# The two-bank PSUM tile gets a place of its own and takes M's first block; the last output tile goes out in two halves

## The chip, the cores and the metric

The kernel runs on one core of one Trainium2 chip. What counts is the device time of one execution in microseconds (us). Several executions were timed, and one more was taken by the hardware profiler. The engines are called as the profile calls them: PE is TensorE (matmuls and transposes), PEld its weight loads, DVE is VectorE, ACT is ScalarE, POOL is GpSimd, and SP (SyncE) issues the DMAs.

## What is computed

Three blocks follow each other: a causal attention with a bias from a running sum, an expert layer of two products, and a second layer with a softmax-weighted activation and a norm.

```python
# q, k, v: (4, 8, 576, 64); s: (4, 8, 576)
scores = scale * q @ k^T                       # causal mask
scores = scores + minimum(-(cum_i - cum_j), 0) # cum = cumsum(max(s, 0))
attn_out = softmax(scores) @ v
x = attn_out as (2304, 512)

a = x @ w1; b = x @ w2                         # w1, w2: (512, 1024)
x = ((a * b) @ w3) @ w_out                     # w3: (1024, 1024), w_out: (1024, 512)

h = x @ w_in                                   # w_in: (512, 1024)
solu = h * softmax(h)
ln = (solu - mean) / sqrt(var + 1e-6) * g_ln
out = ln @ w_out2                              # (2304, 512)
```

The weights come as 64-bit floats and are made 32-bit on the chip.

## The kernel before

**Precision and words.** Every product is made of three matmuls on fp32r parts: a high part (`hi`, a copy on ACT, L93) and a low part (`lo`, a subtraction, L98, on DVE or POOL). Names end in `h` or `l`, or H and L, for the parts. A 64-bit weight block is loaded into `stage`, made 32-bit by `to_f32` (ACT L340, DVE L346, L347, L351), and split by L93 and L98 into `W` (w1 and w2), `w3h`/`w3l`, and so on. `pump` (L393 on) takes converted blocks in turn; inside the attention it is pinned behind the last score reduction and exponential of part 0 (`behind`, set in `softmax_tile`).

**Attention.** A loop over steps (`for st, (h, ph) in enumerate(steps)`, L541 on) does head h's scores in three parts (`qk_part`, matmuls `sc` at L169, L177, L178; DVE reduces with L186, ACT exponentiates with L190), its normalisation (L218, L219, ACT L226, DVE L228), the transposes of an earlier head `ph` (`tr` L247, copied to `PT` by DVE L95 or ACT L93) and the product with v (`av` L275). Two operations per head split q and k into parts `QK` (ACT L93, POOL L98). From step 10 the matmuls of `a` and `b` (units `ab_unit`, L303, 12 matmuls of 288 columns each) fill in between; ACT copies `a` (L315) and DVE multiplies `b` with it into `g_sb` (L323), which goes to DRAM (`g_scr`).

**PSUM.** Up to step 10 there are a pool psA of two tiles of two banks (`bigtile`) and psB of four tiles of one bank (`smalltile`). At step 11 these are let go, and psE (one tile of two banks) and psF (six of one bank) take their place. `bigtile` serves part 0 of a head's scores and `av`; `smalltile` all else. A tile in a new pool can be written when those that lay in its banks have been read.

**M.** The product w3 @ w_out is made once (`m_unit`, eight blocks of 24 matmuls at L626), so that the second half of the kernel multiplies `g` with M (`x`, L710). Each block's high part goes to `MH`, its low part to `ML`. Before, psC (X, Y, Z, W, one bank each) and psD (four banks) are opened behind psE and psF, and M's blocks take psD's. Meanwhile the DVE splits `gl`, words of `w_in` (`IB11l` and so on) and the last blocks of w3.

**The rest.** For each pair of token tiles: `x`, then `h_pair` (`hX`, `hY`, `hZ`, `hW`, L742, a scheme with seven products for eight), softmax, norm, a transpose (by DMA; by PE for the last two tiles), and `out_unit` (`o`, 24 matmuls of 512 columns at L836, one ACT copy, one store of 256 KB). Tile `o` has one buffer.

**Order.** The program is written in the order of these loops, and a scheduler then sets each engine's own queue from its planned times and from the pools. Lines such as

```python
with tc.issue_after(last_tr[0].ins):
```

pin an instruction behind another. So a change of pools can move instructions on PE, DVE, ACT and SP far from the lines that it edits. Inside an engine the queue is executed in order.

Of the kernel before, what the change touches and what calls it, by code (L numbers as in the profile page):

```python
# [8 lines left out]
F32 = mybir.dt.float32  # L9
# [3 lines left out]
AF = mybir.ActivationFunctionType  # L13
ALU = mybir.AluOpType
AX = mybir.AxisListType
PSUM = bass.MemoryType.PSUM
# [10 lines left out]
def tile_attention_moe(  # L27
# [15 lines left out]
    nc = tc.nc  # L43
    B, H, D, _, S = qkT.shape
    NH = B * H
    T, DM = out.shape
# [3 lines left out]
    KF = DF // 128  # L50
# [6 lines left out]
    for i in (2, 3, 1, 4, 0):  # L57
# [3 lines left out]

    dram = ctx.enter_context(tc.tile_pool(name="dram", bufs=1, space=DRAM))
    ps_ctx = ExitStack()
    PSP = [
        ps_ctx.enter_context(tc.tile_pool(name="psA", bufs=2, space=PSUM)),
        ps_ctx.enter_context(tc.tile_pool(name="psB", bufs=4, space=PSUM)),
# [15 lines left out]
    def bigtile(name):  # L82
        return PSP[0].tile([128, 2, 512], F32, tag="A", name=name)

    def smalltile(name):
        return PSP[1].tile([128, 512], F32, tag="B", name=name)

# [404 lines left out]
    for i in range(2):  # L492
# [14 lines left out]
        out=wmask[:, S - 128:S], in_=wmask[:, S - 128:S], pattern=[[-1, 128]],  # L507
# [36 lines left out]
    for st, (h, ph) in enumerate(steps):  # L544
        for _ in range(NF.get(st, 0)):
            fill.extend(ab_unit(*units.pop(0)))
        left = len(fill)
        if st == 11:
            ps_ctx.close()
            PSP[:] = [  # L550
                ps_ctx.enter_context(tc.tile_pool(name="psE", bufs=1, space=PSUM)),
                ps_ctx.enter_context(tc.tile_pool(name="psF", bufs=6, space=PSUM)),
            ]

        def F(share):
            while fill and len(fill) > left * (1 - share):
                fill.pop(0)()

        if h is not None:
            if NQ <= h + 2 < NH:  # L560
                load_head(h + 2)
            qk_part(h, 0)
        if st > 1:
            pump(PUMP.get(st, 0))
        if h is not None:
            qk_part(h, 1)
            qk_part(h, 2)
        F(FS)
        if h is not None:
            normalise(h)  # L570
        if ph is not None:
            for part in range(4):
                tr_part(ph, part)
        if late:
            with tc.issue_after(last_tr[0].ins):
                for fn in late.pop():
                    fn()
        if h is not None:
            if h % 2 == 1:
                load_v(h // 2)  # L580
            if NQ - 2 <= h < NQ:
                t = QK[h % 2] = at.tile([128, 4, S], F32R, tag="QK", bufs=2, name=f"QK{h % 2}")
                aug_rows(t[:, 0], t[:, 3])
            if h + 1 < NH:
                split_qk(h + 1)
            if h + 3 < NQ:
                load_head(h + 3)
                load_aug(h + 3, cumf_scr[h + 3:h + 4])
            if NQ <= h + 2 < NH:
                load_aug(h + 2, cum_scr[h + 2])  # L590
        F(1)
        if ph is not None and ph % 2:
            parts = av_parts(ph // 2)
            if ph < PD or st == len(steps) - 1:
                for fn in parts:
                    fn()
            else:
                late.append(parts)
# [4 lines left out]
    NT = T // 128  # L603
# [15 lines left out]
        w_job(w3L[f, :, 1024 * i:1024 * i + 1024], dst)  # L619

    def m_unit(f):
        ps = smalltile("m")
        for k in range(KF):
            H3, L3 = m_st[f, k // 4]
            for w_, o_ in ((H3, WOH), (H3, WOL), (L3, WOH)):
                nc.tensor.matmul(  # L626
                    ps, w_[:, k % 4], o_[:, k],
                    start=(k == 0 and w_ is H3 and o_ is WOH), stop=(k == KF - 1 and w_ is L3),
                )
        hi(MH[:, f], ps)  # L630
        lo(ML[:, f], ps, MH[:, f])
# [8 lines left out]
    for i in range(8):  # L640
# [8 lines left out]
    behind.clear()  # L649
    right0.close()  # L650
    ps_ctx.close()
    PSP[:] = [
        ctx.enter_context(tc.tile_pool(name="psC", bufs=1, space=PSUM)),
        ctx.enter_context(tc.tile_pool(name="psD", bufs=4, space=PSUM)),
    ]
    HD = DF // 2

    r2 = ctx.enter_context(tc.tile_pool(name="r2", bufs=1, side="right"))
# [39 lines left out]
    def x2_half(c, i):  # L698
        ps = smalltile("x2").rearrange("p (a t) -> p a t", a=2)
        x2_t[c, i] = ps  # L700
        last = None
        for a in range(2):
            m = 2 * i + a
            with ExitStack() as order:
                if last is not None:
                    order.enter_context(tc.issue_after(last.ins))
                for k in range(KF):
                    GH, GL = g_hl[c][k // 2]
                    for w_, g_ in ((MH, GH), (MH, GL), (ML, GH)):
                        last = nc.tensor.matmul(  # L710
                            ps[:, a], w_[:, k, m * 128:m * 128 + 128], g_[:, k % 2],
                            start=(k == 0 and w_ is MH and g_ is GH), stop=(k == KF - 1 and w_ is ML),
                        )
        if i == 1:
            g_hl.pop(c)
# [114 lines left out]

    def out_unit(t):
        LH, LL = lt_t.pop(t)
        ps = smalltile("o")
        for k in range(KF):
            for l_, w_ in ((LH, OH), (LH, OL), (LL, OH)):
                nc.tensor.matmul(  # L836
                    ps, l_[:, k], w_[:, k],
                    start=(k == 0 and l_ is LH and w_ is OH), stop=(k == KF - 1 and l_ is LL),
                )
        o = p2.tile([128, DM], F32, tag="o", bufs=1, name="o")  # L840
        nc.scalar.activation(out=o, in_=ps, func=AF.Copy)
        nc.sync.dma_start(out=out[t * 128:t * 128 + 128], in_=o)

    NCH = NT // 2

    def h_pair(c):
        t0, t1 = 2 * c, 2 * c + 1
        for t in (t0, t1):
            so = p2.tile([128, DF], F32, tag="so", bufs=2, name="so")
            ln_t[t] = so, p2.tile([128, 8], F32, tag="sv", bufs=4, name="sv")  # L850
        h0, h1 = ln_t[t0][0], ln_t[t1][0]
        X, Y, Z, W = (PSP[0].tile([128, HD], F32, tag=n, name=f"h{n}") for n in "XYZW")
        h_mm(X, "A11", "B11", True)
        copy(h0[:, 0:HD], X)
        h_mm(Z, "S1", "T1", True)
        copy(h1[:, HD:], Z)
        h_mm(Y, "A12", "B21", True)
        meet(t0, 0, Y)
        h_mm(X, "S2", "T2", False)
        copy(h0[:, HD:], X)  # L860
        if c + 1 < NCH:
            x2_first(c + 1)
        h_mm(Z, "S4", "B22", False)
        meet(t0, 1, Z)
        ln_exp(t0)
        h_mm(W, "A22", "T4", True)
        h_mm(X, "S3", "T3", False)
        copy(h1[:, 0:HD], X)
        ln_mean(t0)
        meet(t1, 1, X)  # L870
        meet(t1, 0, W)
        ln_exp(t1)
        ln_apply(t0)
# [34 lines left out]
    p2 = ctx.enter_context(tc.tile_pool(name="p2", bufs=1, side="left"))  # L908
    OH = p2.tile([128, KF, DM], F32R, name="OH")
    OL = p2.tile([128, KF, DM], F32R, name="OL")  # L910
    x2_half(0, 0)
    x2_first(0)
    x2_half(0, 1)
# [7 lines left out]
    for c in range(NCH):  # L921
# [8 lines left out]
        last = c == NCH - 1  # L930
# [77 lines left out]
```

## Time and profile before

| | |
|---|---|
| time, median of 3 runs | 732.38 us (731.66 to 733.02) |
| the profiled execution's own time | 732.8 us |
| its span in the trace | 731.1 us |
| mean granted clock of TensorE | 0.995 |
| PE busy | 714.2 us (98%) |
| DVE, ACT, POOL busy | 507.7, 470.4, 95.2 us |
| HBM read, written | 59.04, 20.14 MB |

The span runs from the first to the last event that the profiler saw; the execution's own time has 1.7 us more around it. An engine's busy time is the union of its instructions' times, and for PE the ends of matmuls are modelled, so back-to-back matmuls overlap in the rows: what one costs in a row of its like is the distance of the starts. A wait is put down to the instruction whose end released it last. PEclk is the granted clock as a share of 2.4 GHz.

### The profile page before, as it was taken

The page shows a single profiled execution, that of the slowest core. Times are in us where ns is not written, and L with a number is a line of the kernel's source. Part 1 is how long each engine was busy: PE and PEld are TensorE (multiplying, and loading weights), DVE is VectorE, ACT ScalarE, POOL GpSimd, SP SyncE. Part 2 cuts the span into 40 slices and gives each one's busy share as a digit, 9 for nine tenths or more (in the row PEclk, how much of TensorE's full clock was granted, in tenths as well). Part 3 has the DMA queues.
Part 4 walks back from the last instruction along what each step waited for, and adds up shares of the span by engine and source line. Part 5 has one row for each costly group of instructions (what it writes and reads, how often), then busy time and mean ns, then how long its engine had stood idle before and what let it go on. Part 6 is the DMA issues. An engine that isn't in the chain of part 4 may idle for free.

```text
span 731.1 us, 12896 instructions
## 1 busy us (share of the span) xinstructions
PE 714.2 (98%) x4618; PEld 631.5 (86%) x4618; DVE 507.7 (69%) x1251; ACT 470.4 (64%) x977; POOL 95.2 (13%) x88
## 2 busy tenths in 40 slices
PE   9989998999999999999998999999999999999997
PEld 6669888889899999999997889988888988888886
DVE  7996989898777887822777966675747366563651
ACT  7996878798676777822544735576737465563742
POOL 3051322234121221000000000001000000000000
PEclk9999999999999999999999999999999999999999
DMA  5644555555476655514566933153324252302311
GB/s 124 190 135 132 156 164 146 164 148 127 140 205 184 207 164 175 179 62 161 185 204 201 378 114 101 59 116 87 79 66 102 45 133 68 87 19 68 66 36 43
DMA packets 79827, 95.50 MB, mean 131 GB/s; under 512 B 41418, under 2 KB 52682, under 8 KB 79764
## 3 DMA queue, kind: packets, MB, share of 16 engines
q1 hardware_dynamic: 79764, 94.69, 44.5%
q8 instruction: 36, 0.59, 0.3%
q14 instruction: 27, 0.22, 0.1%
HBM read 59.04 MB, written 20.14 MB: 108 GB/s over the span
## 4 chain that ended last, share of the span: by engine, by line
PE 81%; DVE 9%; DMA 5%; ACT 2%; issue 2%; SPq 0%; DVEq 0%; ACTq 0%
PE x L710 14%; PE o L836 14%; PE a L303 12%; PE b L303 11%; PE av L275 6%; PE hX L742 5%; PE tr L247 5%; DMA stage<-in_w_dram 4%; PE hZ L742 3%; PE sc L178 2%; PE sc L177 2%; PE hW L742 2%; PE hY L742 2%; DVE stage L351 2%; PE sc L169 1%
## 5 line engine op out<-in xcount | busy, mean ns | idle before, releaser
L190 ACT ACTIVATE P<-P,STAT 64x64 f32<-64x64 f32 (+4 forms) x160 | 88.5, 556 | 22.9 <-DVE STAT L186 22.3
L98 POOL TENSOR_TENSOR QK<-qk,QK 64x1152 fp32r<-64x1152 f32 x24 | 66.2, 2759 | 172.9 <-ACT QK L93 172.8
L710 PE MATMUL x<-gl,MH 128*128 128x256 f32 x288 | 80.4, 279 | 0.0
L710 PE MATMUL x<-gh,ML 128*128 128x256 f32 x288 | 80.2, 279 | 0.0
L710 PE MATMUL x<-gh,MH 128*128 128x256 f32 x288 | 79.9, 279 | 0.0
L303 PE MATMUL b<-xT0h,W 128*128 128x288 f32 x256 | 58.4, 301 | 3.5 <-DVE W L98 2.1
L303 PE MATMUL a<-xT0h,W 128*128 128x288 f32 x256 | 59.2, 306 | 0.0
L247 PE MATMUL tr<-ident,P 128*128 128x128 f32 x416 | 54.4, 275 | 3.5 <-DVE STAT L186 2.7
L303 PE MATMUL a<-xT1h,W 128*128 128x288 f32 x256 | 57.6, 300 | 0.0
L836 PE MATMUL o<-OH,lh 128*128 128x512 f32 x144 | 57.0, 396 | 0.2 <-DVE ll L98 0.2
L836 PE MATMUL o<-OH,ll 128*128 128x512 f32 x144 | 57.0, 396 | 0.0
L836 PE MATMUL o<-OL,lh 128*128 128x512 f32 x144 | 57.0, 396 | 0.0
L303 PE MATMUL b<-xT1h,W 128*128 128x288 f32 x256 | 56.4, 295 | 0.0
L710 PEld LDWEIGHTS x<-gl,MH 128*128 128x128 f32 x288 | 54.1, 188 | 1.5 <-DVE gl L98 0.2
L710 PEld LDWEIGHTS x<-gh,MH 128*128 128x128 f32 x288 | 53.9, 188 | 1.1
L710 PEld LDWEIGHTS x<-gh,ML 128*128 128x128 f32 x288 | 54.0, 188 | 0.9
L806 DVE COPY lt<-turned 128x2048 uint16<-128x2048 uint16 x16 | 22.0, 1373 | 45.4 <-DMA turned<-half 45.4
L247 PEld LDWEIGHTS tr<-ident,P 128*128 128x128 f32 x416 | 46.8, 141 | 5.4 <-issue 1.6
L323 DVE TENSOR_TENSOR g_sb<-b,a_sb 128x288 f32<-128x288 f32 x64 | 28.7, 450 | 31.6 <-PE b L303 21.5
L340 ACT ACTIVATE stage<-stage 128x512 f32<-128x512 f32 x56 | 37.1, 679 | 20.5 <-DMA stage<-in_w_dram 18.7
L226 ACT ACTIVATE P<-P,STAT 128x576 f32<-128x576 f32 x64 | 42.7, 717 | 10.5 <-DVE STAT L219 10.4
L315 ACT ACTIVATE a_sb<-a 128x288 f32<-128x288 f32 x64 | 25.7, 403 | 36.3 <-PE a L303 36.0
(191 smaller groups left out, 1984.1 us busy)
## 6 DMA issues: line engine op xcount, KB each, us to landing
stage<-in_w_dram SPq DMA_DIRECT2D x32, 512.0 KB
g_scr<-g_sb SPq DMA_DIRECT2D x32, 288.0 KB
stage<-in_wo_dram SPq DMA_DIRECT2D x16, 512.0 KB
qk<-in_qk_dram SPq DMA_DIRECT2D x24, 288.0 KB
QK<-QK SPq DMA_DIRECT2D x24, 288.0 KB
gl<-g_scr SPq DMA_DIRECT2D x24, 256.0 KB
wf<-wf_scr SPq DMA_DIRECT2D x22, 256.0 KB
out_dram<-o SPq DMA_DIRECT2D x18, 256.0 KB
```

Of the source, the lines that this page charges most:

```text
L98: eng.tensor_tensor(out=dst, in0=src, in1=hi_.bitcast(F32), op=ALU.subtract)
L190: ex = nc.scalar.activation(out=dst, in_=dst, func=AF.Exp, bias=st[0:rows, ti:ti + 1], scale=-1.0, accum_out=st[0:rows, 5 + ti:6 + ti],)
L226: nc.scalar.activation(out=dst, in_=src, func=AF.Copy, scale=r)
L247: last_tr[0] = nc.tensor.transpose(ps[:, 128 * n:128 * n + 128], pt[:, o:o + 128], ident)
L275: nc.tensor.matmul(st["ps"][64 * e:64 * e + 64, 448 + c0:448 + c1], vr[:, j, e], PT[(2 * p + e) % 4][:, o + c0:o + c1], **kw,)
L303: nc.tensor.matmul(ps, w_[:, c, fs], x_[:, c, sl], start=(c == 0 and w_ is WH and x_ is XH), stop=(c == KC - 1 and w_ is WL),)
L315: ab_last[0] = nc.scalar.activation(out=a_sb, in_=ps, func=AF.Copy).ins
L323: ab_last[1] = nc.vector.tensor_tensor(out=g[:, sl], in0=ps, in1=st["a"], op=ALU.mult).ins
L340: nc.scalar.activation(out=high.bitcast(F32), in_=high.bitcast(F32), func=AF.Copy, scale=2.0 ** -112)
L710: last = nc.tensor.matmul(ps[:, a], w_[:, k, m * 128:m * 128 + 128], g_[:, k % 2], start=(k == 0 and w_ is MH and g_ is GH), stop=(k == KF ...
L742: last_h[0] = nc.tensor.matmul(ps, x_[:, k], w_[:, k], start=first and k == 0 and x_ is XH and w_ is WH, stop=k == 1 and x_ is XL, skip_gr ...
L836: nc.tensor.matmul(ps, l_[:, k], w_[:, k], start=(k == 0 and l_ is LH and w_ is OH), stop=(k == KF - 1 and l_ is LL),)
```

## The change

Three things. At step 11 psE is opened at the other end of PSUM (`side="right"`) under a context `big_ctx` of its own, and psF takes the six banks left of it; before, psE lay at the left and psF right of it. M's first block is written to the first bank of the psE tile, and not to a bank of psD; psE stays open until M is done, psC then holds Z and W alone, and X and Y get a pool psG in the place of psE behind M. And `out_unit` makes its last tile (t = 17) in two halves of 256 columns, each with 24 matmuls, a copy of half the width and a store of 128 KB; the second half's matmuls are pinned behind the first's.

```diff
--- before.py
+++ after.py
@@ -61,6 +61,7 @@
 
     dram = ctx.enter_context(tc.tile_pool(name="dram", bufs=1, space=DRAM))
     ps_ctx = ExitStack()
+    big_ctx = ExitStack()
     PSP = [
         ps_ctx.enter_context(tc.tile_pool(name="psA", bufs=2, space=PSUM)),
         ps_ctx.enter_context(tc.tile_pool(name="psB", bufs=4, space=PSUM)),
@@ -548,7 +549,7 @@
         if st == 11:
             ps_ctx.close()
             PSP[:] = [
-                ps_ctx.enter_context(tc.tile_pool(name="psE", bufs=1, space=PSUM)),
+                big_ctx.enter_context(tc.tile_pool(name="psE", bufs=1, space=PSUM, side="right")),
                 ps_ctx.enter_context(tc.tile_pool(name="psF", bufs=6, space=PSUM)),
             ]
 
@@ -619,7 +620,7 @@
         w_job(w3L[f, :, 1024 * i:1024 * i + 1024], dst)
 
     def m_unit(f):
-        ps = smalltile("m")
+        ps = smalltile("m") if f else bigtile("m")[:, 0]
         for k in range(KF):
             H3, L3 = m_st[f, k // 4]
             for w_, o_ in ((H3, WOH), (H3, WOL), (L3, WOH)):
@@ -649,10 +650,9 @@
     behind.clear()
     right0.close()
     ps_ctx.close()
-    PSP[:] = [
-        ctx.enter_context(tc.tile_pool(name="psC", bufs=1, space=PSUM)),
-        ctx.enter_context(tc.tile_pool(name="psD", bufs=4, space=PSUM)),
-    ]
+    psp = {}
+    psp["Z"] = psp["W"] = ctx.enter_context(tc.tile_pool(name="psC", bufs=1, space=PSUM))
+    PSP[1] = ctx.enter_context(tc.tile_pool(name="psD", bufs=4, space=PSUM))
     HD = DF // 2
 
     r2 = ctx.enter_context(tc.tile_pool(name="r2", bufs=1, side="right"))
@@ -830,16 +830,21 @@
 
     def out_unit(t):
         LH, LL = lt_t.pop(t)
-        ps = smalltile("o")
-        for k in range(KF):
-            for l_, w_ in ((LH, OH), (LH, OL), (LL, OH)):
-                nc.tensor.matmul(
-                    ps, l_[:, k], w_[:, k],
-                    start=(k == 0 and l_ is LH and w_ is OH), stop=(k == KF - 1 and l_ is LL),
-                )
         o = p2.tile([128, DM], F32, tag="o", bufs=1, name="o")
-        nc.scalar.activation(out=o, in_=ps, func=AF.Copy)
-        nc.sync.dma_start(out=out[t * 128:t * 128 + 128], in_=o)
+        last = None
+        for c0, c1 in ((0, DM),) if t < NT - 1 else ((0, DM // 2), (DM // 2, DM)):
+            ps = smalltile("o")[:, 0:c1 - c0]
+            with ExitStack() as order:
+                if last is not None:
+                    order.enter_context(tc.issue_after(last.ins))
+                for k in range(KF):
+                    for l_, w_ in ((LH, OH), (LH, OL), (LL, OH)):
+                        last = nc.tensor.matmul(
+                            ps, l_[:, k], w_[:, k, c0:c1],
+                            start=(k == 0 and l_ is LH and w_ is OH), stop=(k == KF - 1 and l_ is LL),
+                        )
+            nc.scalar.activation(out=o[:, c0:c1], in_=ps, func=AF.Copy)
+            nc.sync.dma_start(out=out[t * 128:t * 128 + 128, c0:c1], in_=o[:, c0:c1])
 
     NCH = NT // 2
 
@@ -849,7 +854,7 @@
             so = p2.tile([128, DF], F32, tag="so", bufs=2, name="so")
             ln_t[t] = so, p2.tile([128, 8], F32, tag="sv", bufs=4, name="sv")
         h0, h1 = ln_t[t0][0], ln_t[t1][0]
-        X, Y, Z, W = (PSP[0].tile([128, HD], F32, tag=n, name=f"h{n}") for n in "XYZW")
+        X, Y, Z, W = (psp[n].tile([128, HD], F32, tag=n, name=f"h{n}") for n in "XYZW")
         h_mm(X, "A11", "B11", True)
         copy(h0[:, 0:HD], X)
         h_mm(Z, "S1", "T1", True)
@@ -908,6 +913,8 @@
     p2 = ctx.enter_context(tc.tile_pool(name="p2", bufs=1, side="left"))
     OH = p2.tile([128, KF, DM], F32R, name="OH")
     OL = p2.tile([128, KF, DM], F32R, name="OL")
+    big_ctx.close()
+    psp["X"] = psp["Y"] = ctx.enter_context(tc.tile_pool(name="psG", bufs=1, space=PSUM, side="right"))
     x2_half(0, 0)
     x2_first(0)
     x2_half(0, 1)
```

The scheduler's queues change with it: POOL's order is the same, those of PE, DVE, ACT and SP differ between step 10 and step 20 of the attention, around M, and at the last tile. Three places follow. Lines are one higher in the changed kernel, and a name's number is its tile's.

PE at step 11. `sc_899` is head 9's part 0 (the two-bank tile), `sc_922` its part 1; `sc_957` and `sc_980` are those of head 10. `a_858`, `b_873` and `a_998` are the first of 12 matmuls of their units. Before:

```order
L177 MATMUL sc_899<-QK1_656 128x512
L178 MATMUL sc_899<-QK1_656 128x512
...
L303 MATMUL a_858<-xT0h_130,W00_122 128x288
...
L303 MATMUL b_873<-xT0h_130,W02_124 128x288
...
L177 MATMUL sc_957<-QK0_595 128x512
L178 MATMUL sc_957<-QK0_595 128x512
...
L177 MATMUL sc_922<-QK1_656 128x448
...
L177 MATMUL sc_980<-QK0_595 128x448
...
L303 MATMUL a_998<-xT0h_130,W00_122 128x288
```

and in the changed kernel:

```order
L304 MATMUL a_858<-xT0h_130,W00_122 128x288
...
L304 MATMUL b_873<-xT0h_130,W02_124 128x288
...
L178 MATMUL sc_899<-QK1_656 128x512
L179 MATMUL sc_899<-QK1_656 128x512
...
L178 MATMUL sc_922<-QK1_656 128x448
...
L178 MATMUL sc_980<-QK0_595 128x448
...
L304 MATMUL a_998<-xT0h_130,W00_122 128x288
...
L178 MATMUL sc_957<-QK0_595 128x512
L179 MATMUL sc_957<-QK0_595 128x512
```

`sc_899` has gone behind `a_858` and `b_873`, and `sc_957` from ahead of `sc_922` into `a_998`.

DVE a little later: `W03_125` is the low part of a converted block of w2, `stage_758` and `stage_766` are two blocks on their way, `tr_1050` a bank of transposes, `STAT1_117` and `P_898` the statistics and probabilities of head 9, `b_1013` the unit ahead of `b_1078`. Before:

```order
L186 ISA STAT2_118 128x1
L351 SCALAR_TENSOR_TENSOR stage_766<-stage_766 128x512
L98 TENSOR_TENSOR W03_125<-stage_758,W02_124 128x4x128
L323 TENSOR_TENSOR g_sb_886<-b_1013,a_sb_1011 128x288
L218 TENSOR_SCALAR STAT1_117<-STAT1_117 128x5
L95 COPY PT0_112<-tr_1050 128x512
```

and in the changed kernel:

```order
L187 ISA P_956,STAT2_118<-sc_957,lmask_109 128x576
L187 ISA STAT2_118 128x1
L352 SCALAR_TENSOR_TENSOR stage_758<-stage_758 128x512
L352 SCALAR_TENSOR_TENSOR stage_766<-stage_766 128x512
L219 TENSOR_SCALAR STAT1_117<-STAT1_117 128x5
L220 RECIPROCAL STAT1_117<-STAT1_117 128x5
L229 TENSOR_SCALAR P_898<-P_898,STAT1_117 128x320
L229 TENSOR_SCALAR P_898<-P_898,STAT1_117 128x192
L96 COPY PT0_112<-tr_1050 128x512
L229 TENSOR_SCALAR P_898<-P_898,STAT1_117 64x64
L324 TENSOR_TENSOR g_sb_886<-b_1013,a_sb_1011 128x288
...
L99 TENSOR_TENSOR W03_125<-stage_758,W02_124 128x4x128
```

The reduction of `sc_957` has come behind the others, with both last conversion steps behind it, and head 9's normalisation stands ahead of the copy of `tr_1050`; `W03_125` comes 14 rows behind where the conversion ends.

DVE in M: `gl0` to `gl3` are the low parts of `g`'s first tokens, `ML_4158` the low part of M's first block. Before:

```order
L98 TENSOR_TENSOR gl0_4809<-gl0_4809,gh0_5113 128x512
L98 TENSOR_TENSOR gl1_4810<-gl1_4810,gh1_5116 128x512
L98 TENSOR_TENSOR gl2_4811<-gl2_4811,gh2_5119 128x512
L98 TENSOR_TENSOR ML_4158<-m_4835,MH_4157 128x512
L98 TENSOR_TENSOR gl3_4812<-gl3_4812,gh3_5122 128x512
L98 TENSOR_TENSOR IB11l_4789<-wf_4817,IB11h_4788 128x512
```

and in the changed kernel:

```order
L99 TENSOR_TENSOR gl0_4808<-gl0_4808,gh0_5112 128x512
L99 TENSOR_TENSOR ML_4158<-m_4834,MH_4157 128x512
L99 TENSOR_TENSOR gl1_4809<-gl1_4809,gh1_5115 128x512
L99 TENSOR_TENSOR gl2_4810<-gl2_4810,gh2_5118 128x512
L99 TENSOR_TENSOR gl3_4811<-gl3_4811,gh3_5121 128x512
L99 TENSOR_TENSOR IB11l_4788<-wf_4816,IB11h_4787 128x512
```

`ML` of the first block has moved up by two.

## Rows read from the trace of the kernel before

**Rows 1.** The page, busy time of PE, share of the span, instructions.

```profile
PE 714.2 (98%) x4618; PEld 631.5 (86%) x4618; DVE 507.7 (69%) x1251; ACT 470.4 (64%) x977; POOL 95.2 (13%) x88
```

**Rows 2.** PE's waits from 40 to 480 us: total, times, longest.

```profile
PE tr L247 <- DVE STAT L186: 2.7, 3, 1.4
PE m L626 <- DVE g_sb L323: 2.2, 1, 2.2
PE b L303 <- DVE W L98: 2.1, 1, 2.1
...
PE b L303 <- ACT W L93: 0.8, 1, 0.8
...
PE m L626 <- ACT w3h L93: 0.6, 1, 0.6
```

**Rows 3.** Windows: busy time of each engine, PEclk, DMA share, GB/s.

```profile
40.00:100.00 60.00, 55.24 (x387) 49.02 (x386) 51.09 (x149) 48.73 (x123) 21.62 (x13) 0.97 0.50 141
100.00:130.00 30.00, 27.14 (x190) 25.47 (x189) 24.15 (x65) 23.68 (x53) 6.56 (x3) 0.94 0.52 162
...
392.00:428.00 36.00, 36.00 (x158) 29.58 (x158) 32.02 (x57) 23.95 (x42) 0.00 (x0) 1.00 0.88 308
```

**Rows 4.** Windows of 2 us at the low clock, columns as above.

```profile
94.00:96.00 2.00, 2.00 (x9) 2.00 (x10) 2.00 (x5) 2.00 (x8) 2.00 (x1) 0.50 0.72 218
...
126.00:128.00 2.00, 2.00 (x11) 2.00 (x10) 2.00 (x9) 1.98 (x5) 0.00 (x0) 0.50 0.88 254
```

**Rows 5.** Timeline of PE around 680 us: start, duration, instruction.

```profile
675.62 0.28 PE L710 MATMUL x<-gl,MH 128*128 128x256 f32 x1
...
677.37 0.40 PE L742 MATMUL hX<-IT3h,XWh 128*128 128x512 f32 x1
...
681.79 0.39 PE L836 MATMUL o<-OH,lh 128*128 128x512 f32 x1
...
682.72 0.40 PE L836 MATMUL o<-OL,lh 128*128 128x512 f32 x1
```

**Rows 6.** Timeline of the last 5 us, all engines.

```profile
726.68 0.19 PEld L836 LDWEIGHTS o<-OH,ll 128*128 128x128 f32 x1
726.91 0.40 PE L836 MATMUL o<-OH,ll 128*128 128x512 f32 x1
727.40 0.60 ACT L841 ACTIVATE o<-o 128x512 f32<-128x512 f32 x1 [5.00 <-PE o L836]
728.02 0.33 SPq L842 DMA_DIRECT2D out_dram<-o  x1
```

**Rows 7.** DMA from 726 to 732 us in 40 slices.

```profile
GB/s 0 0 0 0 0 0 0 0 0 0 0 0 0 0 0 0 0 0 0 328 410 410 382 219 0 0 0 0 0 0 0 0 0 0 0 0 0 0 55 0
```

**Rows 8.** Timeline of DVE in M.

```profile
401.98 0.68 DVE L98 TENSOR_TENSOR ML<-m,MH 128x512 fp32r<-128x512 f32 x1
402.58 0.68 DVE L98 TENSOR_TENSOR gl<-gl,gh 128x512 fp32r<-128x512 f32 x1
```

**Rows 9.** Timeline of PE at `b_1078`, with its wait.

```profile
83.53 0.40 PE L303 MATMUL b<-xT0h,W 128*128 128x288 f32 x1 [0.67 <-DVE g_sb L323]
```

**Rows 10.** Timeline of DVE from 79 to 130 us.

```profile
79.97 3.14 DVE L98 TENSOR_TENSOR W<-stage,W 128x512 fp32r<-128x512 f32 x1
...
83.40 0.15 DVE L218 TENSOR_SCALAR STAT<-STAT 128x5 f32<-128x5 f32 x1
83.47 0.68 DVE L95 COPY PT<-tr 128x512 f32<-128x512 f32 x1
...
84.28 0.62 DVE L228 TENSOR_SCALAR P<-P,STAT 128x320 f32<-128x320 f32 x2
...
87.03 0.43 DVE L346 TENSOR_SCALAR stage<-stage 128x512 uint32<-128x512 uint32 x1 [0.96 <-DMA stage<-in_w_dram]
...
129.88 1.84 DVE L346 TENSOR_SCALAR stage<-stage 128x512 uint32<-128x512 uint32 x1 [1.85 <-DMA stage<-in_w_dram]
```

**Rows 11.** Timeline of POOL from 66 to 100 us.

```profile
76.14 6.41 POOL L98 TENSOR_TENSOR QK<-qk,QK 64x1152 fp32r<-64x1152 f32 x2 [12.44 <-ACT QK L93]
```

## The prediction

> **What bounds the kernel now.** I read first the busy shares: TensorE (PE) is busy in 714.2 of 731.1 us [rows 1], so the time is PE's own work, 16.9 us in which it stands, and what a low clock takes. Then the list of PE's waits over the first two thirds [rows 2]: the largest are waits of matmuls for results of VectorE (DVE), 2.7 us of transposes behind the score reductions (1.4 the longest), 2.1 us of a `b` unit for a converted weight, 2.2 us of the first `m` unit, then 0.6 of a later one. Then the stages by window [rows 3]: between 40 and 130 us the clock column is 0.97 and 0.94, in 392 to 428 it is 1.00 and DVE is busy in 32.0 of 36 us. The short windows [rows 4] show that the low clock is two stretches at half (0.50, that is 1.2 of 2.4 GHz), one behind the 1.4 us wait and one behind the 2.1 us wait; 60 us x 0.03 and 30 us x 0.06 make each worth 1.8 us. The 2.24 us stand ahead of `m` was followed by 1.00 [rows 3]. So whatever the change does to the time, it does by moving PE's waits: in the attention, at the start of M, and at the end, where only the last tile's way out is left.
>
> **Part 1, the last tile in two halves.** PE gets 48 matmuls of 256 columns for 24 of 512. In this kernel 15 matmuls of 128x256 start from 675.62 to 677.37, 0.117 us each, and four of 128x512 from 681.79 to 682.72, 0.2325 each [rows 5]. So 48 x 0.117 = 5.60 stands against 24 x 0.2325 = 5.58: PE pays nothing. The Trainium skill, page "TensorE: Matmul & The Clock Gate", section "Back-to-back issue gap", says that in a stream of a weight load per matmul the spacing isn't proportional to the columns (81 ns at 128, 131 ns at 512). By that, read off at 256, the halves would cost about 1.5 times the whole, an estimate of 2.7 us more at the very end; the rows here, with a weight load per matmul too, are proportional, and the measurement decides. What is left behind PE now is a copy of 0.60 us, the store's issue at 728.02 and 0.75 us of packets (five slices of 0.15) in 3.1 us from 728.02 to the end [rows 6, 7]. With the first half's copy and store beside PE's second half (2.8 us of matmuls cover about 2 us of copy, issue and packets; uncovered they would give the gain back), the second half is a copy of 0.30 to 0.45 and 0.35 to 0.5 us of packets; the rest, latency, stays. Gain 0.15 to 0.3 plus 0.25 to 0.4: **-0.6**, bounds -0.3 and -0.8. SP's queue gets one store more at the end, with nothing behind it.
>
> **Part 2, M's first block in the two-bank tile.** `m_unit(0)` no longer opens a bank of a pool that starts when psE and psF are let go, so it doesn't wait for the last multiply `g_sb`; its first matmul comes right behind the last `b`. That removes 2.24 us [rows 2]. Next late are the converted `w3` blocks: the 0.61 us wait of a late `m` matmul for ScalarE's (ACT's) `w3h` [rows 2]. Their chain is a load that follows the `g` store and loads on SP's queue, which don't move, and then DVE, which is nearly full [rows 3] and in the new order has one `ML` earlier by one or two places. An `ML` is 0.68 us, 0.60 to the next row's start [rows 8]; if one or two of them come out from ahead of the chain, the last blocks come 0.6 to 1.2 earlier. PE comes 2.24 earlier, so that wait grows from 0.61 to 0.61 + 2.24 - (0.6 to 1.2) = 1.65 to 2.25. The part is worth 2.24 - (1.04 to 1.64) = 0.6 to 1.2: **-0.9**; bounds 0 (the chain does not move) and -2.2 (it moves as much as PE). After this, `X` and `Y` have a pool of their own, opened behind M; their first use is some hundred `x` matmuls later, so that costs nothing.
>
> **Part 3, the swap of pools in the attention.** This part isn't in the words of the change. psE lies on psB's last banks instead of psA's first, so head 9's big score tile `sc_899` must wait until `b` units have left those banks. The scheduler's order follows: `a_858` and `b_873` go ahead of `sc_899`, and head 10's `sc_957` goes from ahead of `sc_922` to inside the next `a` unit. The same matmuls stand ahead of the next `b_1078`, so PE reaches it at 83.53 - 0.67 = 82.9 [rows 9] plus the wait of `sc_899`: 82.9 to 83.5, say 83.3. Of the two conditions of `b_1078`, the multiply of the unit before is what held it by 0.67; in the new order DVE's `PT` copy of `tr_1050` stands ahead of that multiply, behind two `L351`, `L218`, `L219` and two `L228` of head 9.
>
> What decides is when DVE can do these. Its operations with inputs in SBUF alone were held until a POOL `QK` operation ended: `W` took 3.14 us where the same operation on `ML` takes 0.68 [rows 8, 10], `L346` 1.84 against 0.43 [rows 10]; the two `QK` operations filled 76.14 to 82.55 [rows 11]. In the new order the second waits for `sc_957`, some 25 matmuls later, and for ACT's longer queue, which I lay out at about 2 us: it ends at 84.2 instead of 82.55. From there the held operation needs 0.56 more (79.97 + 3.14 - 82.55), `L218` and the equally small `L219` 0.15 each, two `L228` 0.62, the copy 0.68 [rows 10]: 84.2 + 2.2 = 86.4, with hand-overs 86.6. PE waits 86.6 - 83.3 = 3.3 instead of 0.67: **+2.6**. Both sides: 0 if the second `QK` operation doesn't move and DVE does the short ones ahead of it; with `L351` held as well (two of 0.69) about +4.0. The Trainium skill, page "GPSIMD Engine Reference", section "1. Specifications", tells of contention with VectorE only for instructions in a two-port mode or with two SBUF inputs. No row shows `L228` beside POOL; `L346`, with one tensor input, was held for 1.84 us [rows 10]. If only two-input instructions were touched, `L228` would run through and part 3 would cost about 0.3. I take `L346` as the nearest row.
>
> The next waits (transposes behind reductions, 1.4 us and its low clock) fall on the same chains 2.6 us later, and I leave their sum. Behind them, at 120 to 128 us, before loses 0.8 + 2.1 us of waits [rows 2] and 1.8 of clock for `W` parts that come late. Loads wait for the stage buffers, which the same delay holds back, so I keep 4.4 of these 4.7: **+2.3** for part 3. Its bounds: 2.6 - 4.7 = -2.1, if PE's delay hides these waits whole; and 2.6 + 1.8 = +4.4, if the 3.3 us wait is followed by a half clock of its own.
>
> **Sum.** +2.3 - 0.9 - 0.6 = +0.8 us. The profiled execution took 732.8 us with a span of 731.1; the median of the runs is 732.38, 0.4 below. From the median: **733.2** (733.6 from the profiled execution).
>
> **The rivals.** (a) Faster: PE, 2.6 us late from 83 us on, finds the `W` parts of 120 us already there; neither those waits nor the half clock form. For it: no `W` wait stands in the list behind 130 us [rows 2]. Against it: weight loads follow the same buffers. 732.4 - 2.1 - 0.9 - 0.6 = 728.8, or 729 to 730.9 with half of it. (b) Neutral attention: POOL's second `QK` operation falls beside DVE's PSUM reads, or `L228` runs through it, and only the wait of `sc_899` is left, at most 0.3: 732.4 + 0.3 - 1.5 = 731.2. [...] (c) Slower: the 3.3 us wait brings a third stretch of half clock, and nothing is caught up later: 732.4 + 4.4 - 1.5 = 735.3. It decides from the point at which the copy of `tr_1050` ends past 86; waits of 1.4 and 2.1 us were followed by half clock, the 2.24 us one was not. (d) M gives all back: the `w3h` chain doesn't move, 0.9 fails, 734.1. (e) The change doesn't do what it says, `m_unit(0)` still waits for `g_sb`: its waits in the built order name old loads and `av` only, so little speaks for it; 734.1. (f) PE pays for the halves: a weight load takes 0.19 us [rows 6], longer than a 256-column matmul's 0.117, and if it set the pace the tile would take 48 x 0.19 = 9.1 us instead of 5.6: 733.2 + 3.5 = 736.7; the `x` matmuls, each with such a load, speak against it [rows 5]. The page on TensorE speaks for something of the kind.
>
> **How the numbers follow.** Forecast 0.36, (a) 0.25, (b) 0.11, (c) 0.18, (d) 0.06, (e) 0.02, (f) 0.02. A measurement of this kernel can tell about 0.2%, 1.46 us, from no change: faster is below 730.9, slower above 733.85. The forecast's own spread, 732 to 734.3, puts 0.28 within and 0.08 above; (a) lies below but for 0.01; (b) is half and half; (c) and (f) lie above, (d) and (e) mostly. Faster 0.24 + 0.05 = 0.29; same 0.28 + 0.01 + 0.06 + 0.01 = 0.36; slower 0.08 + 0.18 + 0.07 + 0.02 = 0.35. The range reaches from inside (a) to past (c): 729.5 to 736.0; it leaves out the end of (a) and the sums of high ends, some 2 in 10.
>
> **What would show it.** Right: in the list of waits no `m` on `g_sb`, a wait of `m` on `w3h` near 2 us, a wait of `b` at 83 us on the `PT` copy near 3 us, an end 2.5 us behind the last store's issue. Wrong: no wait over 1 us at 83 us, or the waits of 120 to 128 us gone, or PE's last tile longer than 5.6 us.

## The result and the profile after

The changed kernel takes 738.99 us in the median of six executions (737.29 to 740.46), the kernel before 732.70 (six executions, 731.28 to 734.47): ratio 1.0086, 95% interval 1.0065 to 1.0107. The forecast was 733.2, in a range from 729.5 to 736.0. The profiled execution of the changed kernel took 737.29 us and has a span of 735.2 us.

PE's busy row of the page, in answer to [rows 1]: 2.5 us more of busy time than before, and 1.6 us more in which PE stands (735.2 - 716.7 = 18.5 against 16.9).

```profile
PE 716.7 (97%) x4642; PEld 633.3 (86%) x4642; DVE 508.6 (69%) x1251; ACT 470.4 (64%) x978; POOL 94.4 (13%) x88
```

PE's waits from 40 to 480 us, in answer to [rows 2]: the wait of `m` on `g_sb` has gone, and so has the `b` unit's on DVE's `W`; in their place stand 3.8 us of a `b` unit on a DVE normalisation (`P`, L229 here) and 2.1 us of an `a` unit on a `PT` copy.

```profile
PE b L304 <- DVE P L229: 3.8, 1, 3.8
PE a L304 <- DVE PT L96: 2.1, 1, 2.1
PE b L304 <- ACT W L94: 1.6, 1, 1.6
...
PE x L710 <- ACT gh L94: 0.5, 1, 0.5
PE m L627 <- ACT w3h L94: 0.5, 1, 0.5
```

The windows of the attention, in answer to [rows 3]: PE is busy 52.69 of 60 us (55.24 before) and 25.70 of 30 (27.14 before), 4.0 us less in all, at nearly the same clock.

```profile
40.00:100.00 60.00, 52.69 (x362) 45.77 (x360) 48.42 (x135) 45.57 (x110) 19.63 (x14) 0.97 0.43 125
100.00:130.00 30.00, 25.70 (x175) 23.29 (x176) 24.17 (x65) 22.05 (x54) 6.71 (x3) 0.95 0.56 150
```

PE at `b_1078`, in answer to [rows 9]: 3.76 us where before had 0.67.

```profile
88.53 0.37 PE L304 MATMUL b<-xT0h,W 128*128 128x288 f32 x1 [3.76 <-DVE P L229]
```

How that comes about stands in the timelines of POOL and DVE there, in answer to [rows 10, 11]. Two POOL operations, no longer back to back, each hold a conversion step on DVE: 2.88 us, and 3.73 for two, where one takes 0.68. Between them stands the reduction of `sc_957` (`lmask`), which could not start before 82.42. The copy of `tr_1050`, for which the forecast let `b_1078` wait, ends at 88.38. The profile names the row behind it, the short `L229`, which ends at 88.54; it does not tell the two apart. The low part `W` of the block that is converted there is done at 90.71.

```profile
78.96 2.99 POOL L99 TENSOR_TENSOR QK<-qk,QK 64x1152 fp32r<-64x1152 f32 x1 [14.21 <-ACT QK L94]
83.25 3.03 POOL L99 TENSOR_TENSOR QK<-qk,QK 64x1152 fp32r<-64x1152 f32 x1 [1.30 <-ACT QK L94]
```

```profile
78.74 0.68 DVE L348 SCALAR_TENSOR_TENSOR stage<-stage 128x512 uint32<-128x512 uint32 x1
...
79.62 2.88 DVE L348 SCALAR_TENSOR_TENSOR stage<-stage 128x512 uint32<-128x512 uint32 x1
82.42 0.74 DVE L187 CUSTOM_DVE_ANT_0 P<-sc,lmask 128x576 f32<-128x576 f32 x1
...
83.09 3.73 DVE L352 SCALAR_TENSOR_TENSOR stage<-stage 128x512 uint32<-128x512 uint32 x2
...
87.69 0.69 DVE L96 COPY PT<-tr 128x512 f32<-128x512 f32 x1
...
90.06 0.65 DVE L99 TENSOR_TENSOR W<-stage,W 128x512 fp32r<-128x512 f32 x1
```

At the end, in answer to [rows 6]: the last copy is 0.38 us instead of 0.60, and from the last store's issue to the end are 735.19 - 732.38 = 2.8 us instead of 3.1.

```profile
731.97 0.38 ACT L846 ACTIVATE o<-o 128x256 f32<-128x256 f32 x1 [2.40 <-PE o L842]
732.38 0.33 SPq L847 DMA_DIRECT2D out_dram<-o  x1
```

Stage by stage, from the starts of PE's instructions in the two profiled executions (first `a` or `b` matmul, last one, first `hX`, last transpose, end):

| stage | before | after | difference |
|---|---|---|---|
| to the first `a` | 59.03 | 60.06 | +1.0 |
| first to last `a`, `b` | 330.44 | 335.19 | +4.8 |
| M and the first `x` | 58.56 | 56.92 | -1.6 |
| pairs of tiles | 267.35 | 267.75 | +0.4 |
| last transpose to the end | 15.75 | 15.26 | -0.5 |

The first row scatters between executions of kernels that are the same up to there (59.03 to 60.79 in all traces of this study but e2_mown's, which has 64.10), and so does the third; the experiments tell what of this is the change.

### The profile page after: what moved, and what is told of

Read it like the earlier page. It is cut to its first block, busy times and chain, and to the rows that moved or that the text cites. A ratio compares the mean times of both kernels' runs of the same rounds, so it can differ in the third digit from the quotient of the medians.

```text
span 735.2 us, 12955 instructions
## 1 busy us (share of the span) xinstructions
PE 716.7 (97%) x4642; PEld 633.3 (86%) x4642; DVE 508.6 (69%) x1251; ACT 470.4 (64%) x978; POOL 94.4 (13%) x88
## 4 chain that ended last, share of the span: by engine, by line
PE 79%; DVE 10%; DMA 6%; ACT 3%; issue 2%; SPq 0%; DVEq 0%; ACTq 0%
PE o L842 14%; PE x L710 13%; PE a L304 12%; PE b L304 11%; PE av L276 5%; PE hX L742 5%; DMA stage<-in_w_dram 5%; PE tr L248 5%; PE hZ L742 3%; PE sc L179 2%; PE sc L178 2%; DVE stage L352 2%; DVE P L187 2%; DVE stage L348 2%; PE hW L742 2%; PE hY L742 2%
## 5 line engine op out<-in xcount | busy, mean ns | idle before, releaser
L191 ACT ACTIVATE P<-P,STAT 128x576 f32<-128x576 f32 (+4 forms) x160 | 88.3, 553 | 26.2 <-DVE STAT L187 25.6
L304 PE MATMUL a<-xT0h,W 128*128 128x288 f32 x256 | 61.1, 311 | 2.8 <-DVE PT L96 2.1
L842 PE MATMUL o<-OH,lh 128*128 128x512 f32 (+1 forms) x152 | 58.4, 384 | 0.2 <-DVE ll L99 0.2
L842 PE MATMUL o<-OH,ll 128*128 128x512 f32 (+1 forms) x152 | 58.3, 383 | 0.0
L842 PE MATMUL o<-OL,lh 128*128 128x512 f32 (+1 forms) x152 | 58.3, 383 | 0.0
L276 PE MATMUL av<-PT,VT 128*64 128x64 f32 (+4 forms) x384 | 48.8, 394 | 0.0
```

The lines of the kernel that those rows point to most:

```text
L191: ex = nc.scalar.activation(out=dst, in_=dst, func=AF.Exp, bias=st[0:rows, ti:ti + 1], scale=-1.0, accum_out=st[0:rows, 5 + ti:6 + ti],)
L276: nc.tensor.matmul(st["ps"][64 * e:64 * e + 64, 448 + c0:448 + c1], vr[:, j, e], PT[(2 * p + e) % 4][:, o + c0:o + c1], **kw,)
L304: nc.tensor.matmul(ps, w_[:, c, fs], x_[:, c, sl], start=(c == 0 and w_ is WH and x_ is XH), stop=(c == KC - 1 and w_ is WL),)
L842: last = nc.tensor.matmul(ps, l_[:, k], w_[:, k, c0:c1], start=(k == 0 and l_ is LH and w_ is OH), stop=(k == KF - 1 and l_ is LL),)
```

## Experiments

Four ways of cutting the change come first. Each kernel was timed in turn with the kernel before on one chip; its ratio, with a 95% interval, is to the runs of before in that comparison. It is not the quotient of the two medians; the two differ by up to 0.0015. The kernel before has medians from 731.99 to 733.97 us in these comparisons, so kernels of different comparisons are set against each other by what each takes above its own before: first by the medians, then by the ratios.

**The last tile alone.** In before, `out_unit` as in the change.

> Before, with only the last output tile in two halves; every queue up to the last tile is before's. Theory (the tail gains by its smaller last copy and store, PE pays nothing): about 0.5 us below before, from the last matmul's start to the end 3.5 us instead of 4.2. Rival (a 256-column stream with a weight load per matmul runs slower than half a 512-column one): the last 48 matmuls take 8 to 9 us instead of 5.6, 2.5 to 3.5 us above before.

Measured: 733.95 us against 733.12, ratio 1.0001 (0.9980 to 1.0021), so nothing that the time can tell. The trace has the part by itself: from the last transpose to the end 15.31 us. Over all traces of this study the stretch is 15.64 to 15.96 us with a whole tile (ten kernels) and 15.26 to 15.32 with halves (six). The theory holds at a smaller size, about -0.4; the rival falls.

**M's first block alone.** psE in a context of its own on its old side, psC and psD opened on the other side, `bigtile` for block 0:

```diff
-                ps_ctx.enter_context(tc.tile_pool(name="psE", bufs=1, space=PSUM)),
+                big_ctx.enter_context(tc.tile_pool(name="psE", bufs=1, space=PSUM)),
...
-        ps = smalltile("m")
+        ps = smalltile("m") if f else bigtile("m")[:, 0]
```

> Before, with only M's first block in the two-bank tile, which stays on the side that it has in before (the pools opened behind it go to the other side instead); the attention's queues are before's word for word, M's are those of the changed kernel. Theory (the 2.24 us wait goes, part of it comes back at the last converted blocks): 1.2 to 1.6 us below before, no wait of m on g_sb, one of about 0.5 us on w3h. Rival (the chain of loads and conversions sets the end of M): a wait on w3h of 2.5 us or more, time as before.

Measured: 733.36 against 733.12, ratio 0.9994 (0.9972 to 1.0015). No wait of `m` on `g_sb`, but 1.6 us on `w3h` and 0.5 of `x` on `gh`. The rival is nearer. From the last `a` or `b` matmul to the first `hX` this kernel takes 58.07 us, and the five others with the new order of M 56.92 to 58.71, mean of the six 57.8; the kernels with the old order take 57.41 to 58.56, mean of nine 57.9 (a tenth, x2b_unpin, has 60.06 with a half clock in it). The pairs behind take 267.72 to 267.77 with the new order and 267.35 to 267.53 with the old, 0.3 more. So this part is worth nothing that can be told.

**The pool's side alone.** In before, `side="right"` for psE at step 11, let go together with psF.

> Before, with only the two-bank tile's pool opened at the other side of PSUM at step 11; the attention's queues are the changed kernel's word for word, M's and the tail's are before's. Theory (all of the loss comes from this order): 5 to 8 us above before, a wait of b of about 3.8 us near 84 us, and head 13's first transposes 5 us later than in before. Rival (the loss lies in M or is of the start of the execution): within 1.5 us of before.

Measured: 740.48 against 733.12, which is 7.4 us by the medians and 6.2 by the ratio 1.0085 (1.0053 to 1.0118). The whole loss is here. PE's waits from 62 to 140 us of this kernel:

```profile
PE b L304 <- DVE P L229: 3.8, 1, 3.8
PE a L304 <- DVE PT L96: 2.3, 1, 2.3
PE b L304 <- ACT W L94: 1.6, 1, 1.6
```

**The other two parts without it.**

> M's first block in the two-bank tile and the last tile in halves, with the two-bank tile on before's side: the changed kernel without its attention order. Theory (the two parts add): 1.7 to 2.1 us below before, about 730.5. Rival (M's gain is given back behind it): about 0.5 us below before, the tail's alone.

Measured: 733.71 against 733.12, ratio 1.0002 (0.9979 to 1.0025): the rival, or less. PE's waits from 380 to 480 us show where M's gain went in the profiled execution:

```profile
PE m L627 <- ACT w3h L94: 2.1, 2, 1.9
PE x L710 <- ACT gh L94: 0.6, 1, 0.6
```

**Banks or order?** In the changed kernel, psA at the right too, so that psE finds psA's banks:

> The changed kernel, with the attention's first big pool psA at the right side too, so that the two-bank tile of step 11 lies on a bank pair of psA as in before; every queue is word for word that of e4_mown_tail. Theory (what costs is whose readers the tile must wait for, not which banks it has): as e4_mown_tail, within 0.3% of before. Rival (the upper banks themselves, or where psF lies, cost): 738 us or more.

Measured: 732.34 against 732.70, ratio 1.0002 (0.9984 to 1.0020). With psE still at the right end, the loss is gone. It does not lie in the banks themselves: with psE in the same ones, only whose readers the tile waits for, and the order that the scheduler makes of that, are back as before.

**The held stretches.** In e3_side, one line more, which leaves POOL's operation out for two heads:

```diff
+        if h not in (11, 12):
             lo(t[64:128, 1::2], raw, t[64:128, 0::2], G)
```

> The run before with only the pool's side (e3_side), with POOL's low-part operation left out for heads 11 and 12, so that these heads' scores lack the low part of q and k; PE's queue is e3_side's past the stalled b unit, DVE's up to the converted weight behind it. Theory (two POOL operations hold DVE's operations on SBUF, each about 3 us): no DVE operation of 2.5 us or more between 75 and 90 us, the wait of b of 3.8 us falls to 1.5 or less, the time 3 to 5 us below e3_side. Rival (the new order of DVE's queue is late by itself): that wait stays at 3 us or more, the time within 1.5 us of e3_side.

Measured: 734.53 us against 732.70, ratio 1.0027 (1.0011 to 1.0043): above before by 5.5 us less than e3_side by the medians, 4.3 by the ratios. DVE has nothing of 2.5 us from 75 to 90 us. `b_1078` waits 1.19 us, and no longer for DVE but for ACT's part of the converted weight:

```profile
85.96 0.40 PE L305 MATMUL b<-xT0h,W 128*128 128x288 f32 x1 [1.19 <-ACT W L94]
```

The weights are still late. PE waits for them three times up to 140 us, and their low parts are done 3.5, 7.7, 6.5 and 6.4 us later than in before, where the changed kernel has 7.6, 10.8, 13.1 and 10.5 for the same blocks (both executions start their first `a` 1.0 us later than before's).

```profile
PE b L305 <- ACT W L94: 3.8, 3, 1.6
```

The same in the kernel before, as a control:

> The kernel before with POOL's low-part operation left out for heads 11 and 12 (their scores lack the low part of q and k); the queues of PE, DVE and ACT are before's word for word. The control for x1_skip. Theory (in before the same two operations fall beside score reductions that read PSUM and hold one converted weight for 2.5 us, which cost PE 0.7 us): 0 to 2 us below before, so that the step from e3_side to x1_skip is the new order's and not the operations' alone. Rival (the two operations cost as much in any order): 4 us or more below before.

Measured: 733.63 against 733.97, ratio 0.9996 (0.9978 to 1.0014). The two operations cost before nothing that can be told, and 4.3 to 5.5 us in the new order; the part on the clock says how much of that is half clock.

**The work or the holding?** In e3_side, the two operations on DVE (`V if h in (11, 12) else G`):

> e3_side with the low-part operation of heads 11 and 12 made by DVE in place of POOL; nothing is left out. Theory (what costs is the holding, not the work): DVE has two operations of 1.2 to 1.3 us more and none of 2.5 us or more between 75 and 90 us, the wait of b near 84 us falls to 2 us or less, the time 2 to 5 us below e3_side. Rival (DVE's queue is simply too long there): the wait stays above 3 us and the time within 1.5 us of e3_side.

Measured: 736.41 against 733.97, ratio 1.0039 (1.0025 to 1.0053): 4.9 us less above before than e3_side by the medians, 3.4 by the ratios, though DVE does 2 x 1.36 us more. As expected; but there is a wait of a transpose at 121 us (2.7 us on `g_sb`), so the order keeps a price of its own.

**One at a time.** With `if h != 11`, and with `if h != 12`:

> e3_side with POOL's low-part operation left out for head 11 alone (its scores lack that part); all other queues are e3_side's word for word. Theory (the first operation holds a conversion step ahead of the reduction of sc_957, and so delays the reduction, ACT's next copy of q and k, and the second POOL operation): that reduction 2 to 3 us earlier than in e3_side, the wait of b 1 to 2.5 us in place of 3.8, the time 2 to 4 us below e3_side. Rival (only the second one counts): the wait stays above 3 us, the time within 1 us of e3_side.

Measured: 737.72 against 731.99, ratio 1.0069 (1.0045 to 1.0092): 1.6 us less above before than e3_side by the medians, 1.2 by the ratios. That is less than the 2 to 4 expected, and the intervals overlap, so the time does not tell it from e3_side. The reduction starts at 80.09 instead of 81.99, and the wait of `b_1078` is 1.2 us, for ACT's `W` as in x1_skip. The second POOL operation starts as late as it did (83.13 against 82.83): that part of the theory falls. It now holds another DVE operation, the short last `L228` of head 9 (L230 in this kernel), for 2.19 us instead of 0.24:

```profile
83.64 2.19 DVE L230 TENSOR_SCALAR P<-P,STAT 64x64 f32<-64x64 f32 x1
```

```profile
83.13 2.65 POOL L99 TENSOR_TENSOR QK<-qk,QK 64x1152 fp32r<-64x1152 f32 x1 [18.53 <-ACT QK L94]
```

> e3_side with POOL's low-part operation left out for head 12 alone; all other queues are x1_skip's word for word. Theory (the two add, the second held the last conversion steps ahead of the copy for which b waits): the wait of b 1.5 us or less, the time 1 to 3 us above x1_skip and 3 to 5 below e3_side. Rival (the first alone sets the end): within 1 us of e3_side.

Measured: 735.00 against 731.99, ratio 1.0037 (1.0023 to 1.0050): 4.4 us less above before than e3_side by the medians, 3.5 by the ratios, and 1.2 or 0.7 more than x1_skip. `b_1078` waits 1.3 us, put down to `L228`; a later `b`, at 124 us, waits 1.0 on the copy. The first operation alone costs little; the second costs most. The queues differ between these two kernels, so the two numbers are not parts of one sum.

**The pin.** In e3_side, the pin of `pump` taken away for steps 11 to 16:

```diff
+            if 11 <= st <= 16:
+                behind.clear()
             pump(PUMP.get(st, 0))
```

> e3_side with the weight conversions of steps 11 to 16 no longer pinned behind the reduction and the exponential of a head's first score tile. Theory (the pin carries the late score tile over to the conversions, and these set the pace up to 148 us): ACT's conversion of the sixth block starts within 1.5 us of before's 72.5 us, the wait of b falls to 1.5 us or less, the time is within 2 us of before. Rival (the loss comes from the late score tiles themselves, not from the conversions): 738 us or more.

Measured: 735.57 against 732.70, ratio 1.0046 (1.0027 to 1.0065): 4.5 us less above before than e3_side by the medians, 2.9 by the ratios. The sixth block's conversion starts at 72.7 us, as in before, and its low part is done at 77.6 (before 83.1, e3_side 90.3). So the pin carried the late score tile over to the weights, and without it about half of the loss or more is gone. Some 3 us are left, more than the 2 expected, with waits of 1.5 us on ACT's `a_sb`, 1.6 on a reduction, and 1.7 of a score matmul for which the profile names nothing. POOL still holds DVE in this kernel (a conversion step of 2.89 us at 78.87). Control:

> The kernel before with the same pin taken away in steps 11 to 16: the control for x2b_unpin, and a try at a faster kernel. Theory (in before the pinned score tile comes early, so the pin costs nothing there): within 2 us of before either way. Rival (the pin costs in any order): 2 us or more below before.

Measured: 731.36 against 732.70, ratio 0.9989 (0.9974 to 1.0004): the pin costs before nothing that can be told.

**A better kernel?** The two parts that don't lose, with the pin off:

> e4_mown_tail (M's first block in the two-bank tile, the last tile in halves, before's attention) with the pin of steps 11 to 16 taken away as in x2c_unpin_before. Theory (the gains add): 0.5 to 1 us below x2c_unpin_before, 1.5 to 3 us below before, few stretches of half clock. Rival (x2c's distance from before was scatter): within 1 us of before.

Measured: 733.72 against 733.97, ratio 1.0001 (0.9985 to 1.0018): the rival holds. And with the pin off to the end of the attention:

> The same with the pin taken away from step 11 to the end of the attention. Theory (from step 17 on PE waits for nothing in before, so that the pin there costs nothing and its absence can only put conversions ahead of reductions): within 1 us of x4_best. Rival (conversions ahead of the reductions delay the exponentials and PE's transposes): 2 us or more above x4_best.

Measured: 749.37 against 733.97, ratio 1.0224 (1.0200 to 1.0249): far worse. Where before PE waits for nothing from 160 to 345 us, this kernel has

```profile
PE sc L178 <- DVE xT0l L99: 4.4, 3, 2.2
PE sc L178 <- issue: 3.1, 1, 3.1
```

so the pin has its worth in the later steps. No kernel of this study beats the one before by more than the measurement can tell.

**The clock.** Each run's mean granted clock gives what half clock took at most: (1 - clock) x span, as a mean over the runs of a kernel. Where PE would have stood anyway, half clock costs less.

| kernel | us that half clock took | runs |
|---|---|---|
| before (each comparison) | 2.6 to 2.8 | 18 to 35 |
| e1_tail, e2_mown, e4_mown_tail, x3_psA_right, x6_before_skip | 2.4 to 2.8 | 12 each |
| the changed kernel | 4.5 | 6 |
| e3_side | 4.8 | 6 |
| x9_skip11 | 3.4 | 7 |
| x10_skip12 | 1.0 | 12 |
| x1_skip | 0.7 | 12 |
| x5_dve_lo | 1.3 | 12 |
| x2b_unpin | 3.1 | 12 |
| x4_best | 1.7 | 12 |
| x2c_unpin_before | 0.8 | 12 |
| x8_best_all | 6.6 | 5 |

So some 2 of the changed kernel's 6 us are the clock's. Of what the two POOL operations cost, the share is larger: from e3_side to x1_skip the half clock falls from 4.8 to 0.7 us, 4.1 of the 4.3 to 5.5 us. The traces say it less sharply: there half clock between 55 and 385 us takes 3.4 and 0 us, and PE's waits in that stretch sum to 10.0 and 7.5 us, where five kernels with the old order (before, e1_tail, e4_mown_tail, x3_psA_right, x6_before_skip) have 5.2 to 6.8. The kernels with the longest single waits of PE lose most (3.8 us in the changed kernel and e3_side, 3.1 in x8_best_all), those without a wait of 2 us least; x5_dve_lo, with 2.7 us and 1.3 lost, does not fit, and no run sets a wait without changing more, so that the waits bring the half clock is not shown.

## Why the prediction was wrong, step by step

| term | forecast | measured | from |
|---|---|---|---|
| last tile | -0.6 | -0.4 | 15.66 and 15.29, medians of the traces with and without halves |
| M | -0.9 | +0.2 | 57.9 to 57.8, and 267.5 to 267.75 |
| attention | +2.3 | +5.7 | 335.8, mean of two traces with the new order (the changed kernel, e3_side); 330.1, of five with the old |
| sum | +0.8 | +5.5 | time: +6.3, interval 4.8 to 7.8 |

The old order's five are before, e1_tail, e4_mown_tail, x3_psA_right and x6_before_skip; e2_mown is left out, since its first `a` came 5 us late. In these traces PE's waits from 55 to 385 us are 3.8 us longer with the new order (9.7 against 5.9), and half clock takes 1.4 us more (3.4 against 2.0).

**The last tile.** Right, but for its size. PE pays a little: eight matmuls of 256 columns from 728.11 to 729.06 are 0.119 us each, not 0.117, so 0.1 us for the tile. It is not the 1.5 times of the estimate from the two figures of the Trainium skill, page "TensorE: Matmul & The Clock Gate", section "Back-to-back issue gap"; rival (f) falls, and the measurement decides. The copy gained 0.22, the store 0.3.

**M.** The mechanism was right, that the wait for `w3h` grows, and rival (d), that M gives all back, was the case. Two sizes were off. The 2.24 us that the change takes away was one execution's: other executions with the old order wait 1.0 (e1_tail), 1.2 (x6_before_skip) and 1.7 (e3_side) there. And a wait of `x` for `gh`, 0.5 to 0.6 us, which before doesn't have, was not in the sum.

**The attention.** The step to `b_1078` was right in kind and nearly in size: a wait of 3.3 us was forecast and 3.76 measured, by the chain of DVE that was named, behind a POOL operation that ends at 86.28, where 84.2 was laid out and before had 82.55. That the wait came out so near is in part luck: PE too arrived later, at 84.77 instead of 83.3, of which 1.0 us is the later start of this execution's first `a`. Three steps of part 3 failed.

First, only one held stretch was counted. The trace has two, and the first, on `L347` of a conversion (L348 here), stands ahead of the reduction of `sc_957` and puts it off by some 2 us (x9_skip11: 80.09 against 81.99). And one condition of `b_1078` was not in the forecast at all: ACT's part of `W`, done at 85.88 in the changed kernel, for which `b_1078` waits 1.2 us in x1_skip and x9_skip11, where POOL's holds are gone from ahead of it. It is late by the pin of `pump` (x2b_unpin).

Second, "the next waits fall on the same chains 2.6 us later, and I leave their sum" was the largest miss. The conversions of weights are a loop: two stage buffers, each load issued when the low part of the block two before it is done. From the traces, the low parts that were done in before at 83.1, 95.4, 105.8 and 125.9 us are done 7.6, 10.8, 13.1 and 10.5 later in the changed kernel, and not 2.6. (The blocks between these are 3.8 to 9.2 later.) The next POOL operations hold DVE again (at 99 and 116 us), and PE stands 1.56 us at 103.84 for a weight and 2.10 at 127.35 for a bank. x1_skip shows that the two operations make up about half of this delay, and x2b_unpin that the pin has a share: without it the sixth block is done at 77.6.

Third, the clock. The extra half clock was put at the upper end (+4.4) and into rival (c), with a chance of 0.18; it is what happens: 4.5 us in the mean instead of 2.7. The profiled executions alone do not show it; each of the two has 3.4 us of it in the attention. Rival (c) named this mechanism, at 735.3 us; its price lacked the loop's delay. That the range ended at 736.0 follows from the same sum.

**`L228` beside POOL.** The forecast took it to be held, from the row of `L346`. x9_skip11 shows it: 2.19 us instead of 0.24. But "operations with inputs in SBUF alone were held until a POOL `QK` operation ended" reads the rows too widely: in before two such operations, at 94.11 and 94.70 us, run through in 0.67 and 0.68 beside a POOL operation that starts at 93.97; that one takes 3.93 us, where six others take 2.64 to 2.68. The Trainium skill, page "GPSIMD Engine Reference", section "1. Specifications", names a two-port mode and two SBUF inputs as what contends; `L228` has one tensor input, so a reading by two inputs alone is wrong here. Whether it runs in such a mode, no trace tells.

**What was also said.** "No `m` on `g_sb`": so it is. "A wait of `m` on `w3h` near 2 us": 0.5 in the profiled execution, 1.3 to 2.1 in e2_mown, e4_mown_tail, x3_psA_right and x4_best. An end 2.5 us behind the last store's issue: 2.8. "Wrong: ... the waits of 120 to 128 us gone": the changed kernel has 0.22 and 2.10 us there against 0.8 and 2.1, but for `g_sb` and a `PT` copy; the waits for `W` that the forecast carried over are gone from there. A remainder is left: x1_skip is still 1.8 us above before, and that with 2.1 us less of half clock than before, so some 3.9 us are the new order's without the two operations; x2b_unpin, with them and without the pin, is 2.9 above. No kernel has neither, so it stays open how much of this is the pin's and how much the late score tiles'.

## What to carry to other kernels

Where a scheduler sets the queues, a change of a buffer's place is a change of order: look whose readers the buffer now waits for, and what is pinned behind the instruction that waits. Where one engine's operation holds another engine's, a delay of 2 us need not stay 2 us; if what is held feeds a loop of loads and conversions, follow that loop for a few turns before calling the rest unchanged, and look at the granted clock over many executions, since half clock can be most of what a hold costs. And a wait that a change removes should be read in more than one execution, with what becomes late next.

## What the runs showed of the hardware

A DVE operation on SBUF that is held beside a POOL operation ends a little behind POOL's end, and the longer it is by itself, the further behind: 0.55 us for one that takes 0.68 by itself (79.62 + 2.88 = 82.50, POOL 78.96 + 2.99 = 81.95), 0.05 us for one of 0.24 (x9_skip11: 83.64 + 2.19 = 85.83, POOL 83.13 + 2.65 = 85.78). Reductions from PSUM run through at their 0.34 to 0.75 us.

Which stretches run at half clock differs between executions: the traces of three kernels with the same attention queues have two, one and none of them between 60 and 140 us (before, e4_mown_tail, x3_psA_right), at granted clocks of 0.50, and the kernel before has mean clocks from 0.992 to 1.000 in its runs. So one execution does not give a kernel's half clock; the means of the table above are over 5 to 35.
